# A new hand-written order for an attention and mixture-of-experts kernel on one core

## The chip, the core and the metric

One core of one Trainium2 chip runs the whole program in one launch. The metric is device microseconds of that launch, as the median of several runs. Engines are named as the profile names them: PE is TensorE's matmuls, PEld its weight loads, DVE is VectorE, ACT is ScalarE, POOL is GpSimd, SP is the engine that starts most of the DMA transfers.

## The reference

Three layers follow one another. All arrays are float32.

```python
# 1. attention: batch 4, 8 heads, 576 positions, head width 64, each query sees 64 keys
scores = (q @ k.T) / 8, masked to 0 <= i - j < 64, minus the row's maximum
attn   = exp(scores) / (sum + 1e-9)
x      = (attn @ v), heads side by side          # 2304 tokens x 512
# 2. a dense layer of width 2048
h = x @ w_in
x = (max(h, 0) + alpha * min(h, 0)) @ w_out      # 2304 x 512
# 3. eight experts of width 1024, the best one for each token
e   = argmax(x @ w_gate), gate = softmax(x @ w_gate)[e]
out = gate * (max(x @ w1[e], 0) @ w2[e])
```

## The kernel before, in words

Float32 products are made of three matmuls on a pair of a rounded operand ("hi") and the rest ("lo"): hi by hi, hi by lo and lo by hi. So each operand is first split by two instructions, a rounding copy and a subtraction.

The tokens are 18 tiles of 128, in five blocks of 4, 4, 4, 3 and 3 tiles. One attention *group* is half of the heads of one tile, so a block of 4 tiles needs groups 0 to 7, the next one groups 8 to 15, and so on up to 35. The dense layer runs block by block, over 16 slices f of 128 of its width. Its 16 weight tiles (`wcat`, 1 MB each, both weight matrices of a slice) are loaded once, and each is prepared once by six instructions before block 0 can use it. The experts' part follows after the last block.

**The order is written out by hand.** `PLAN` (line 29) is a list of tokens, a letter and a number, and `play` (line 834) issues one step for each. Every engine executes its own instructions in the order in which they stand there, and waits at the first one whose operands are not ready. The plan covers blocks 0 to 3; the last block and the experts have loops of their own. The tokens:

- `X`g loads group g's queries, keys and values (SP, line 248); `W`f loads weight tile f (SP, line 179); `c` loads constants.
- `S`g scores (PE, line 279, with two mask matmuls before it, line 273); `x`g row maxima (DVE, 290); `y`g scales them by 1/8 (294); `e`g four exponentials (ACT, 301); `q`g adds epsilon to the sums (309); `r`g reciprocal (DVE, 313); `n`g normalises the probabilities (DVE, 321, or four instructions on ACT, 319); `T`g transposes them (PE, 327); `P`g copies them out of PSUM (337); `O`g multiplies them with the values (PE, 351); `H`g and `L`g split the result into hi (ACT, 337) and lo (DVE, 364).
- `0`f to `5`f prepare weight tile f: `0` scales its exponent words (ACT, 191), `1`, `2`, `3` put the bits together (DVE, 195, 199, 203), `4` rounds to hi (ACT, 337), `5` subtracts for lo (DVE, 211). So `13` is step 1 of tile 3 and `110` step 1 of tile 10.
- In block j, with i = 16 j + f: `s`i is the first product of slice f (PE, 376 to 378, 12 matmuls), `R`, `t` its activation (ACT 391, DVE 395), `h`, `l` the split of that (ACT 337, DVE 401), `u`i the second product (PE, 418 to 420).
- `B`n is n matmuls whose result nobody reads (PE, line 261), `b8` the eight at the very start.
- `Z`, `N`, `D`, `G`, `J`, `j`, `M`, `I`, `i` belong to the routing of finished blocks; `N` loads a row of the gate's weights (`wge`, SP, line 465), `D` is a product with it (DVE, 474).

A suffix names the engine where it is not the usual one: `d` DVE, `p` POOL, `a` ACT. The usual engine of `y`, `q` and `n` is DVE, that of `P` is ACT.

What ties the steps together beyond their data: from group 8 on, `S`, `T` and `O` share two PSUM banks (`aslot`, `give`): `S` takes both and `e` gives them back, `T` takes one until `P`, `O` takes one until `L`. `s` has two banks (`h`), so s2 waits for t0. `raw` has two buffers, so X7 waits for O0 and X9 for O7. Weight tile 8 is loaded over the raw words of tile 0, so W8 waits for `50`.

```python
    def w_low(f):
        lo, hi = wpart(f)
        DVE.tensor_scalar(out=lo, in0=lo, scalar1=29, scalar2=None, op0=ALU.logical_shift_right)
    def out_lo(g):
        xh, xl = xt_part(g)
        DVE.tensor_tensor(out=xl, in0=ob.pop(g).rearrange(...), in1=f32(xh), op=ALU.subtract)
        give(("O", g))
```

Of the kernel before, what the change touches and what calls it, by code (L numbers as in the profile page):

```python
# [28 lines left out]
PLAN = """
c0 X0 b8 X1 c1 S0 X2 B2 x0 S1 y0 C0 e0 W0 B7 x1 y1 e1 S2 q0 r0 X3 n0 x2 T0 B2 P0d y2p X4 00 q1 O0 r1 n1 e2 10 T1 X5 S3  # L30
20 B2 P1d W1 H0 S4 q2p x3 O1 L0 y3p r2 e3 B2 n2 X6 x4 T2 B2 P2d y4p 30 O2 H1 q3p X7 e4 S5 L1 r3 B3 n3 W2 x5 T3 H2 q4p
S6 40 P3d y5p L2 O3 r4 e5 n4 B1 W3 x6 T4 B2 P4d y6p 50 O4 H3 q5p e6 X8 S7 L3 B3 r5 n5 W4 x7 T5 H4 q6p B4 01 L4 y7p P5d
r6 e7 O5 n6 W5 11 T6 B7 21 H5 q7p P6 31 W6 02 O6 L5 B4 r7 H6 n7 41 L6 T7 12 W7 B7 03 51 P7 22 04 O7 W8 B7 32 H7 05 L7
42 13 s0 X9 23 06 52 07 W9 S8 33 R0 s1 08 t0 W10 x8 h0 43 14 y8p s2 l0 e8 53 24 W11 u0 R1 q8p 34 09 r8 t1 44 W12 15 S9
n8a 54 s3 h1 x9 010 l1 y9p 25 R2 u1 e9 t2 35 s4 16 h2 q9p 45 r9 l2 26 n9a T8 55 u2 P8 R3 36 011 t3 46 O8 17 T9 27 X10
H8 s5 h3 P9 L8 l3 012 56 R4 O9 37 u3 H9 X11 L9 47 t4 18 h4 S10 57 s6 l4 x10 R5 t5 y10p e10 u4 28 38 h5 q10p 19 S11 48
r10 l5 s7 n10a 58 x11 W13 R6 29 y11p u5 e11 t6 39 h6 q11p T10 110 49 s8 l6 r11 P10 n11 R7 59 013 O10 t7 W14 u6 H10 210
h7 L10 310 X12 T11 s9 l7 410 111 P11 510 R8 014 t8 O11 211 u7 H11 X13 h8 L11 311 S12 112 411 l8 s10 x12 R9 511 y12p
e12 t9 u8 212 h9 q12p 312 S13 r12 412 n12 s11 l9 512 R10 t10 W15 u9 x13 h10 113 y13p e13 213 s12 l10 313 R11 q13p 015
r13 n13 T12 413 t11 u10 114 P12 513 h11 214 O12 T13 H12 X14 l11 s13 P13 L12 R12 314 t12 414 O13 115 h12 u11 514 X15  # L40
H13 L13 215 S14 l12 s14 315 R13 x14 415 t13 y14p e14 u12 515 h13 q14p r14 S15 n14 l13 s15 x15 R14 t14 y15p e15 u13 h14
q15p r15 n15 T14 l14 T15 P14 u14 P15 R15 t15 h15 O14 l15 O15 H14 X16 u15 L14 H15 L15 X17 s16 Z0 Z1 N0 Z2 N1 Z3 S16 R16
s17 D0 t16 x16 h16 s18 l16 y16 R17 D1 e16 t17 u16 D2 D3 h17 q16 N2 r16 n16 S17 D4 s19 l17 x17 R18 y17 t18 e17 u17 D5
D6 D7 h18 T16 q17 N3 r17 l18 s20 P16 n17 R19 D8 D9 O16 D10 u18 H16 X18 D11 L16 t19 N4 D12 h19 T17 D13 s21 P17 l19 D14
R20 D15 t20 O17 N5 u19 D16 h20 X19 H17 D17 L17 D18 D19 S18 s22 l20 N6 x18 R21 y18 t21 e18 u20 D20 D21 D22 h21 S19 q18
r18 n18 s23 l21 x19 R22 u21 y19 D23 e19 t22 N7 D24 D25 s24 h22 q19 r19 n19 l22 D26 R23 T18 D27 T19 P18 u22 t23 P19 D28
h23 D29 D30 O18 l23 O19 H18 X20 D31 R24 u23 L18 H19 t24 X21 L19 h24 G0 s25 S20 l24 s26 x20 R25 y20 t25 e20 u24 h25 q20
r20 n20 S21 l25 s27 x21 R26 y21 t26 e21 u25 h26 q21 r21 n21 T20 J0 l26 P20 s28 j0 R27 O20 u26 H20 X22 L20 M0 t27 T21
I0 P21 s29 i0 h27 M1 l27 R28 O21 t28 I1 H21 X23 u27 L21 h28 i1 S22 l28 s30 x22 R29 y22 t29 e22 u28 h29 q22 r22 n22 S23
l29 s31 x23 R30 y23 t30 e23 u29 h30 q23 r23 n23 T22 l30 T23 P22 u30 P23 R31 t31 h31 O22 l31 O23 H22 X24 u31 L22 H23  # L50
L23 X25 s32 Z4 Z5 N8 Z6 N9 Z7 S24 R32 s33 D32 t32 x24 h32 s34 l32 y24 R33 D33 e24 t33 u32 D34 D35 h33 q24 N10 r24 n24
S25 D36 s35 l33 D37 R34 D38 t34 u33 D39 h34 x25 N11 y25 s36 D40 e25 l34 D41 D42 R35 T24 q25 u34 r25 P24 n25 t35 D43
h35 D44 N12 O24 l35 T25 H24 X26 D45 s37 R36 P25 L24 D46 D47 t36 O25 N13 u35 D48 h36 X27 H25 D49 L25 D50 D51 S26 s38
l36 N14 x26 R37 y26 t37 e26 u36 D52 D53 D54 h37 S27 q26 r26 l37 s39 n26 R38 D55 t38 N15 D56 u37 h38 D57 D58 D59 s40
l38 x27 R39 t39 u38 y27 h39 D60 e27 D61 D62 s41 l39 D63 R40 q27 r27 n27 T26 t40 u39 P26 G1 h40 O26 T27 H26 X28 s42 P27
L26 l40 R41 t41 O27 h41 u40 X29 H27 L27 S28 l41 s43 x28 R42 y28 t42 e28 u41 h42 q28 r28 n28 J1 l42 T28 j1 s44 R43 P28
O28 u42 H28 X30 M2 L28 t43 I2 s45 h43 i2 M3 l43 R44 I3 u43 t44 i3 h44 S29 l44 s46 x29 R45 y29 t45 e29 u44 h45 q29 r29
n29 s47 l45 R46 t46 h46 T29 u45 P29 O29 l46 H29 X31 u46 R47 L29 t47 h47 s48 l47 u47 R48 t48 h48 S30 Z8 l48 s49 Z9 x30
N16 Z10 N17 Z11 y30 u48 e30 D64 D65 s50 D66 R49 q30 r30 n30 S31 t49 D67 s51 h49 l49 N18 x31 R50 u49 t50 y31 h50 D68
e31 s52 l50 D69 D70 u50 D71 R51 q31 N19 r31 n31 T30 t51 T31 D72 P30 s53 P31 D73 h51 D74 l51 O30 D75 R52 O31 X32 H30  # L60
t52 u51 H31 L30 h52 L31 X33 D76 s54 D77 l52 N20 D78 R53 u52 D79 t53 N21 h53 D80 S32 l53 s55 x32 R54 y32 D81 u53 e32
D82 D83 t54 N22 S33 q32 h54 r32 s56 n32 l54 x33 R55 u54 y33 D84 e33 D85 D86 D87 T32 q33 N23 r33 P32 n33 O32 t55 T33
D88 h55 X34 s57 H32 l55 P33 L32 R56 D89 t56 O33 D90 u55 h56 X35 H33 D91 L33 D92 S34 l56 s58 x34 R57 u56 y34 t57 e34
D93 D94 s59 D95 h57 q34 r34 l57 n34 S35 R58 t58 u57 x35 h58 s60 y35 l58 e35 G2 u58 R59 T34 P34 t59 J2 q35 O34 h59 r35
n35 s61 H34 l59 L34 R60 j2 u59 T35 P35 t60 O35 M4 h60 s62 H35 L35 l60 I4 R61 u60 i4 t61 M5 h61 s63 l61 R62 t62 u61 h62
I5 l62 i5 u62 R63 t63 h63 l63
"""
# [977 lines left out]
```

## Time and profile before

| | |
|---|---|
| median of 3 runs (lowest, highest) | 781.07 us (781.02, 781.63) |
| the profiled execution's own time | 780.53 us |
| its span, first to last instruction | 778.7 us |
| PE busy | 759.4 us (98%) |
| PEld, DVE, ACT, POOL busy | 611.9, 622.6, 461.3, 76.6 us |
| granted TensorE clock, mean | 0.997 of full speed |
| matmuls and their records | 4590 |

The program runs attention for block 0 first (to about 38 us), then the dense layer of blocks 0 to 3 with the attention of the next block in between, then the last block (to about 478 us) and the experts. A PE that is shown busy is not always at its peak, since a matmul's pipeline is counted in; how far apart matmuls start says more. Times in timelines are the start from the span's begin and the length of one group of instructions; in square brackets stands the idle time before it and who ended it.

### The profile page before, as it was taken

What the parts mean: (1) busy time and instruction counts of PE and PEld (TensorE: products, weight loads), DVE (VectorE), ACT (ScalarE), POOL (GpSimd) and SP (SyncE); (2) the same over time, 40 slices, a digit from 0 to 9 for tenths busy, and PEclk for the clock granted to TensorE, in tenths of its full rate; (3) what the DMA queues carried; (4) which work ended last, traced back from release to release, by engine and by line L of the source; (5) the groups of instructions that cost most, each with busy time, mean ns of one, the idle gap of its engine ahead of it and who ended that gap; (6) DMA issues with size and microseconds to landing.
All of it is one profiled execution on the core that took longest, in us unless ns stands there. A gap on an engine that the chain in (4) does not pass through costs nothing.

```text
span 778.7 us, 12731 instructions
## 1 busy us (share of the span) xinstructions
PE 759.4 (98%) x4590; PEld 611.9 (79%) x4595; DVE 622.6 (80%) x1267; ACT 461.3 (59%) x892; POOL 76.6 (10%) x80
## 2 busy tenths in 40 slices
...
GB/s 362 406 355 75 156 82 75 76 92 65 130 75 101 29 129 103 65 65 27 117 89 109 48 48 136 216 178 27 41 281 247 28 218 293 264 257 248 194 88 51
DMA packets 24259, 109.91 MB, mean 141 GB/s; under 512 B 3006, under 2 KB 3390, under 8 KB 17024
## 3 DMA queue, kind: packets, MB, share of 16 engines
...
HBM read 154.09 MB, written 10.26 MB: 211 GB/s over the span
## 4 chain that ended last, share of the span: by engine, by line
PE 81%; DVE 9%; DMA 6%; issue 2%; ACT 1%; SPq 0%; DVEq 0%
PE acc L737 12%; PE h L376 8%; PE acc L418 8%; PE acc L419 8%; PE acc L420 8%; PE h L377 8%; PE h L378 8%; DVE hl L819 4%; PE h L709 4%; PE h L711 4%; PE h L710 4%; DMA hl<-in_wcat_dram 2%; PE att L351 2%; DMA hl<-in_qkv_dram 2%; PE att L279 2%
## 5 line engine op out<-in xcount | busy, mean ns | idle before, releaser
L819 DVE TENSOR_TENSOR hl<-hl,hl 128x1024 fp32r<-128x1024 f32 x176 | 211.2, 1222 | 16.7 <-ACT hl L813 16.0
L813 ACT CAST hl<-hl 128x1024 fp32r<-128x1024 f32 x176 | 180.2, 1049 | 3.6 <-DMA hl<-in_wx_dram 2.6
L737 PE MATMUL acc<-hl,xl 128*128 128x512 f32 x504 | 130.7, 400 | 2.5 <-DVE xl L724 2.5
L376 PE MATMUL h<-xh,hl 128*128 128x512 f32 (+1 forms) x320 | 122.9, 384 | 0.8 <-DVE g L395 0.8
L378 PE MATMUL h<-xh,hl 128*128 128x512 f32 (+1 forms) x320 | 118.0, 369 | 0.0
L377 PE MATMUL h<-xl,hl 128*128 128x512 f32 (+1 forms) x320 | 118.0, 369 | 0.0
L419 PE MATMUL acc<-hl,gl 128*128 128x512 f32 x288 | 112.9, 392 | 0.4 <-DVE gl L401 0.4
L420 PE MATMUL acc<-hl,gh 128*128 128x512 f32 x288 | 112.8, 392 | 0.0
L391 ACT ACTIVATE g<-h 128x512 f32<-128x512 f32 (+1 forms) x80 | 44.6, 558 | 112.7 <-DVE gl L401 99.2
L418 PE MATMUL acc<-hl,gh 128*128 128x512 f32 x288 | 109.8, 401 | 0.0
L737 PEld LDWEIGHTS acc<-hl,xl 128*128 128x128 f32 x504 | 91.2, 188 | 21.4 <-DVE xl L724 3.8
L401 DVE TENSOR_TENSOR gl<-g,gh 128x512 fp32r<-128x512 f32 (+1 forms) x80 | 50.8, 636 | 58.9 <-PE acc L419 54.1
...
L474 DVE SCALAR_TENSOR_TENSOR dot<-stage,wge 128x512 bf16<-128x512 f32 x96 | 66.0, 688 | 10.0 <-DMA wge<-in_wgt_dram 7.6
L337 ACT CAST gh<-g 128x512 fp32r<-128x512 f32 (+1 forms) x80 | 46.5, 581 | 45.9 <-DVE g L395 42.8
L376 PEld LDWEIGHTS h<-xh,hl 128*128 128x128 f32 x320 | 60.1, 188 | 14.0 <-issue 4.0
L395 DVE SCALAR_TENSOR_TENSOR g<-g,beta,h 128x512 f32<-128x512 f32 (+1 forms) x80 | 55.0, 688 | 16.3 <-ACT g L391 16.1
L709 PE MATMUL h<-hl,xh 128*128 128x512 f32 x168 | 67.6, 403 | 0.0
L378 PEld LDWEIGHTS h<-xh,hl 128*128 128x128 f32 x320 | 60.1, 188 | 8.1
L711 PE MATMUL h<-hl,xh 128*128 128x512 f32 x168 | 66.1, 393 | 0.4 <-DVE xh L697 0.2
L377 PEld LDWEIGHTS h<-xl,hl 128*128 128x128 f32 x320 | 60.2, 188 | 7.4
L710 PE MATMUL h<-hl,xh 128*128 128x512 f32 x168 | 65.5, 390 | 0.0
...
## 6 DMA issues: line engine op xcount, KB each, us to landing
...
```

What stands on the lines that cost most here:

```text
L376: PE.matmul(out=h[:, 0:n], lhsT=w_in_op(f, k, 0), rhs=xh[:, k, :], start=(k == 0), stop=False)
L377: PE.matmul(out=h[:, 0:n], lhsT=w_in_op(f, k, 0), rhs=xl[:, k, :], start=False, stop=False)
L378: PE.matmul(out=h[:, 0:n], lhsT=w_in_op(f, k, 1), rhs=xh[:, k, :], start=False, stop=(k == 3))
L418: PE.matmul(out=a, lhsT=gh[:, c0:c0 + 128], rhs=w_out_op(f, 0), start=(f == 0), stop=False)
L419: PE.matmul(out=a, lhsT=gl[:, c0:c0 + 128], rhs=w_out_op(f, 0), start=False, stop=False)
L420: PE.matmul(out=a, lhsT=gh[:, c0:c0 + 128], rhs=w_out_op(f, 1), start=False, stop=(f == 15))
L709: PE.matmul(out=o, lhsT=th[:, k, :], rhs=wh, start=(k == 0), stop=False)
L710: PE.matmul(out=o, lhsT=th[:, k, :], rhs=wl, start=False, stop=False)
L711: PE.matmul(out=o, lhsT=tl[:, k, :], rhs=wh, start=False, stop=(k == 3))
L737: PE.matmul(out=o, lhsT=x[:, f % 4, :], rhs=w[:, lo, (f % 2) * 512:(f % 2) * 512 + 512], start=(x is th and f == 0 and lo == 0), stop=(x i ...
L813: ACT.copy(out=t[:, 0, :], in_=r)
L819: eng.tensor_tensor(out=t[:, 1, :], in0=r, in1=f32(t[:, 0, :]), op=ALU.subtract)
```

## The change

Nothing but the text of `PLAN` changes: 1141 tokens become 1137, and nearly all of them up to the end of block 3 stand in a new order (the five last alone keep their place). By kinds:

- `y`2 to `y`15 and `q`2 to `q`15 (14 and 14 instructions of 128x4) go from POOL to DVE.
- `P`1 to `P`5, copies of 128x512, go from DVE to ACT (`P`0 stays on DVE).
- `n`11 to `n`14 go from DVE to ACT. With `n`8, `n`9 and `n`10, which were there, seven normalisations are on ACT.
- Of the `B` matmuls, 55 in 15 tokens become 51 in 11 (`b8` stays).
- All else is order. The diff, cut to its first lines and to those that the text speaks of:

```diff
-c0 X0 b8 X1 c1 S0 X2 B2 x0 S1 y0 C0 e0 W0 B7 x1 y1 e1 S2 q0 r0 X3 n0 x2 T0 B2 P0d y2p X4 00 q1 O0 r1 n1 e2 10 T1 X5 S3
-20 B2 P1d W1 H0 S4 q2p x3 O1 L0 y3p r2 e3 B2 n2 X6 x4 T2 B2 P2d y4p 30 O2 H1 q3p X7 e4 S5 L1 r3 B3 n3 W2 x5 T3 H2 q4p
-S6 40 P3d y5p L2 O3 r4 e5 n4 B1 W3 x6 T4 B2 P4d y6p 50 O4 H3 q5p e6 X8 S7 L3 B3 r5 n5 W4 x7 T5 H4 q6p B4 01 L4 y7p P5d
-r6 e7 O5 n6 W5 11 T6 B7 21 H5 q7p P6 31 W6 02 O6 L5 B4 r7 H6 n7 41 L6 T7 12 W7 B7 03 51 P7 22 04 O7 W8 B7 32 H7 05 L7
-42 13 s0 X9 23 06 52 07 W9 S8 33 R0 s1 08 t0 W10 x8 h0 43 14 y8p s2 l0 e8 53 24 W11 u0 R1 q8p 34 09 r8 t1 44 W12 15 S9
-n8a 54 s3 h1 x9 010 l1 y9p 25 R2 u1 e9 t2 35 s4 16 h2 q9p 45 r9 l2 26 n9a T8 55 u2 P8 R3 36 011 t3 46 O8 17 T9 27 X10
...
-h7 L10 310 X12 T11 s9 l7 410 111 P11 510 R8 014 t8 O11 211 u7 H11 X13 h8 L11 311 S12 112 411 l8 s10 x12 R9 511 y12p
...
-D82 D83 t54 N22 S33 q32 h54 r32 s56 n32 l54 x33 R55 u54 y33 D84 e33 D85 D86 D87 T32 q33 N23 r33 P32 n33 O32 t55 T33
...
-D93 D94 s59 D95 h57 q34 r34 l57 n34 S35 R58 t58 u57 x35 h58 s60 y35 l58 e35 G2 u58 R59 T34 P34 t59 J2 q35 O34 h59 r35
-n35 s61 H34 l59 L34 R60 j2 u59 T35 P35 t60 O35 M4 h60 s62 H35 L35 l60 I4 R61 u60 i4 t61 M5 h61 s63 l61 R62 t62 u61 h62
...
+c0 X0 b8 X1 c1 S0 X2 B2 x0 S1 y0 C0 e0 W0 B7 x1 y1 e1 S2 q0 r0 n0 X3 x2 T0 B3 P0d X4 00 q1 O0 r1 n1 H0 y2 T1 10 e2 X5
+S3 L0 20 B4 W1 x3 P1 S4 q2 r2 O1 n2 y3 H1 T2 x4 X6 e3 B8 L1 y4 30 X7 P2 S5 q3 r3 n3 e4 O2 11 W2 T3 x5 B2 y5 H2 S6 q4
+r4 P3 n4 e5 W3 O3 L2 x6 T4 B3 y6 12 H3 S7 X8 P4 q5 L3 e6 r5 O4 n5 x7 T5 W4 B6 y7 13 H4 q6 P5 L4 r6 e7 O5 n6 W5 T6 B7
+H5 q7 r7 P6 n7 W6 01 O6 L5 14 T7 H6 B3 21 P7 40 O7 L6 W7 B6 31 H7 02 L7 50 S8 41 X9 22 s0 03 W8 51 04 x8 05 s1 y8 32
+R0 W9 e8 t0 23 33 h0 S9 42 l0 43 q8 u0 r8 52 R1 x9 n8a W10 t1 s2 y9 h1 53 e9 l1 W11 24 u1 R2 q9 r9 34 06 W12 n9a t2 T8
+15 s3 25 P8 h2 35 44 O8 l2 45 T9 X10 54 u2 H8 R3 L8 P9 t3 07 55 O9 h3 s4 16 X11 H9 l3 08 L9 26 09 u3 36 R4 010 t4 46
...
+e11 t6 W13 19 h6 q11 T10 r11 29 n11a s8 l6 P10 39 R7 013 O10 t7 u6 110 X12 H10 h7 210 49 L10 310 T11 P11 l7 410 O11 59
...
+l54 T32 D84 R55 u54 P32 t55 D85 h55 D86 O32 s57 l55 H32 X34 D87 R56 L32 t56 N23 S33 D88 h56 u55 x33 s58 y33 l56 e33
+D89 D90 u56 D91 R57 q33 r33 n33 S34 t57 D92 s59 h57 l57 x34 R58 u57 y34 t58 e34 D93 s60 D94 D95 h58 q34 r34 T33 n34
+P33 l58 T34 G2 O33 R59 P34 u58 X35 H33 O34 H34 L33 L34 J2 t59 j2 s61 h59 l59 S35 M4 R60 u59 x35 y35 t60 e35 s62 h60
+q35 r35 I4 n35 l60 T35 i4 u60 R61 M5 P35 t61 O35 h61 I5 l61 H35 s63 L35 R62 i5 t62 h62 u61 l62 u62 R63 t63 h63 l63
```

## Rows read from the trace of the kernel before

**Rows 1.** Busy time by stretch: PE, PEld, DVE, ACT, POOL, then PE clock, DMA share, GB/s.

```profile
10.00:45.00 35.00, 31.73 (x352) 19.85 (x355) 32.52 (x60) 26.53 (x78) 2.90 (x12) 1.00 1.01 411
...
60.00:120.00 60.00, 60.00 (x394) 47.05 (x393) 55.08 (x74) 37.90 (x83) 5.85 (x8) 1.00 0.31 104
120.00:380.00 260.00, 260.00 (x1709) 208.84 (x1708) 175.88 (x472) 98.94 (x280) 0.91 (x4) 1.00 0.25 84
```

**Rows 2.** Timeline of PE: first and third matmul of s0, S8, then the first of s1 and s3.

```profile
38.65 0.58 PE L376 MATMUL h<-xh,hl 128*128 128x512 f32 x1
...
39.30 0.39 PE L378 MATMUL h<-xh,hl 128*128 128x512 f32 x1
...
41.59 0.39 PE L273 MATMUL att<-c 128*128 128x256 bf16 x2
...
42.51 0.50 PE L376 MATMUL h<-xh,hl 128*128 128x512 f32 x1
...
52.89 0.50 PE L376 MATMUL h<-xh,hl 128*128 128x512 f32 x1 [0.55 <-DVE g L395]
```

**Rows 3.** Timeline of SP: transfers issued: two rows of the gate, then X7.

```profile
8.67 1.85 SPq L465 DMA_DIRECT2D wge<-in_wgt_dram  x2
13.16 0.33 SPq L248 DMA_DIRECT2D raw<-in_qkv_dram  x1
```

**Rows 4.** Timeline of ACT: steps 05 and 06, and the normalisation n8a.

```profile
38.30 1.19 ACT L191 ACTIVATE hl<-hl 128x1024 f32<-128x1024 f32 x1 [0.50 <-DMA hl<-in_wcat_dram]
...
40.80 1.19 ACT L191 ACTIVATE hl<-hl 128x1024 f32<-128x1024 f32 x1 [0.28 <-DMA hl<-in_wcat_dram]
...
53.19 1.28 ACT L319 ACTIVATE sm<-sm,rs 128x128 f32<-128x128 f32 x4
```

**Rows 5.** Timeline of DVE: r0; x6; then n7, L6, 12, 51, 22, 32.

```profile
10.04 0.18 DVE L313 RECIPROCAL rs<-rs 128x4 f32<-128x4 f32 x1
...
23.95 0.75 DVE L290 TENSOR_REDUCE nm<-acc 128x2 f32<-128x256 f32 x2
...
33.85 0.69 DVE L321 TENSOR_TENSOR sm<-sm,rs 128x512 f32<-128x512 f32 x1
34.46 0.42 DVE L364 TENSOR_TENSOR xl<-att,xh 128x256 fp32r<-128x256 f32 x1
34.80 0.68 DVE L195 TENSOR_SCALAR hl<-hl 128x1024 int32<-128x1024 int32 x1
35.40 1.22 DVE L211 TENSOR_TENSOR hl<-hl,hl 128x1024 fp32r<-128x1024 f32 x1
36.53 1.22 DVE L199 SCALAR_TENSOR_TENSOR hl<-hl 128x1024 int32<-128x1024 int32 x1
37.78 1.23 DVE L203 SCALAR_TENSOR_TENSOR hl<-hl 128x1024 int32<-128x1024 int32 x1
```

**Rows 6.** Timeline of PE: T8 with u2 behind it; T32 with O32; O34 behind T34.

```profile
61.23 0.60 PE L327 MATMUL att<-c,sm 128*128 128x128 f32 x4
61.59 0.47 PE L418 MATMUL acc<-hl,gh 128*128 128x512 f32 x1
...
389.04 0.60 PE L327 MATMUL att<-c,sm 128*128 128x128 f32 x4
390.31 0.69 PE L351 MATMUL att<-pt,raw 128*64 128x64 f32 x16 [0.68 <-ACT pt L337]
...
412.13 0.69 PE L351 MATMUL att<-pt,raw 128*64 128x64 f32 x16 [0.34 <-ACT pt L337]
```

**Rows 7.** Timeline of PE: fillers at the start, and two more a little later.

```profile
1.32 3.60 PE L261 MATMUL h<-zero 128*128 128x512 bf16 x8 [1.32 <-POOL one L853]
...
6.42 0.61 PE L261 MATMUL h<-c 128*128 128x512 bf16 x2
```

**Rows 8.** Busy time by stretch at the end, columns as in Rows 1.

```profile
770.00:772.00 2.00, 1.22 (x6) 0.66 (x4) 2.00 (x4) 1.72 (x4) 1.27 (x1) 1.00 0.00 0
...
774.00:776.00 2.00, 0.00 (x0) 0.00 (x0) 0.18 (x1) 0.00 (x0) 0.00 (x0) 0.57 0.47 137
```

More of the change, by code (lines that the diff above doesn't have):

```diff
@@ L35 @@
-n8a 54 s3 h1 x9 010 l1 y9p 25 R2 u1 e9 t2 35 s4 16 h2 q9p 45 r9 l2 26 n9a T8 55 u2 P8 R3 36 011 t3 46 O8 17 T9 27 X10
-H8 s5 h3 P9 L8 l3 012 56 R4 O9 37 u3 H9 X11 L9 47 t4 18 h4 S10 57 s6 l4 x10 R5 t5 y10p e10 u4 28 38 h5 q10p 19 S11 48
-r10 l5 s7 n10a 58 x11 W13 R6 29 y11p u5 e11 t6 39 h6 q11p T10 110 49 s8 l6 r11 P10 n11 R7 59 013 O10 t7 W14 u6 H10 210
-h7 L10 310 X12 T11 s9 l7 410 111 P11 510 R8 014 t8 O11 211 u7 H11 X13 h8 L11 311 S12 112 411 l8 s10 x12 R9 511 y12p
-e12 t9 u8 212 h9 q12p 312 S13 r12 412 n12 s11 l9 512 R10 t10 W15 u9 x13 h10 113 y13p e13 213 s12 l10 313 R11 q13p 015
@@ L40 @@
[L40 to L59, printed above, removed]
@@ L60 @@
-e31 s52 l50 D69 D70 u50 D71 R51 q31 N19 r31 n31 T30 t51 T31 D72 P30 s53 P31 D73 h51 D74 l51 O30 D75 R52 O31 X32 H30
-t52 u51 H31 L30 h52 L31 X33 D76 s54 D77 l52 N20 D78 R53 u52 D79 t53 N21 h53 D80 S32 l53 s55 x32 R54 y32 D81 u53 e32
-D82 D83 t54 N22 S33 q32 h54 r32 s56 n32 l54 x33 R55 u54 y33 D84 e33 D85 D86 D87 T32 q33 N23 r33 P32 n33 O32 t55 T33
-D88 h55 X34 s57 H32 l55 P33 L32 R56 D89 t56 O33 D90 u55 h56 X35 H33 D91 L33 D92 S34 l56 s58 x34 R57 u56 y34 t57 e34
-D93 D94 s59 D95 h57 q34 r34 l57 n34 S35 R58 t58 u57 x35 h58 s60 y35 l58 e35 G2 u58 R59 T34 P34 t59 J2 q35 O34 h59 r35
@@ L65 @@
-n35 s61 H34 l59 L34 R60 j2 u59 T35 P35 t60 O35 M4 h60 s62 H35 L35 l60 I4 R61 u60 i4 t61 M5 h61 s63 l61 R62 t62 u61 h62
-I5 l62 i5 u62 R63 t63 h63 l63
+c0 X0 b8 X1 c1 S0 X2 B2 x0 S1 y0 C0 e0 W0 B7 x1 y1 e1 S2 q0 r0 n0 X3 x2 T0 B3 P0d X4 00 q1 O0 r1 n1 H0 y2 T1 10 e2 X5
+S3 L0 20 B4 W1 x3 P1 S4 q2 r2 O1 n2 y3 H1 T2 x4 X6 e3 B8 L1 y4 30 X7 P2 S5 q3 r3 n3 e4 O2 11 W2 T3 x5 B2 y5 H2 S6 q4
+r4 P3 n4 e5 W3 O3 L2 x6 T4 B3 y6 12 H3 S7 X8 P4 q5 L3 e6 r5 O4 n5 x7 T5 W4 B6 y7 13 H4 q6 P5 L4 r6 e7 O5 n6 W5 T6 B7
@@ new lines @@
+H5 q7 r7 P6 n7 W6 01 O6 L5 14 T7 H6 B3 21 P7 40 O7 L6 W7 B6 31 H7 02 L7 50 S8 41 X9 22 s0 03 W8 51 04 x8 05 s1 y8 32
+R0 W9 e8 t0 23 33 h0 S9 42 l0 43 q8 u0 r8 52 R1 x9 n8a W10 t1 s2 y9 h1 53 e9 l1 W11 24 u1 R2 q9 r9 34 06 W12 n9a t2 T8
+15 s3 25 P8 h2 35 44 O8 l2 45 T9 X10 54 u2 H8 R3 L8 P9 t3 07 55 O9 h3 s4 16 X11 H9 l3 08 L9 26 09 u3 36 R4 010 t4 46
+17 S10 27 h4 s5 011 l4 x10 012 y10 56 e10 u4 37 18 R5 q10 s6 r10 47 t5 28 n10a 57 S11 h5 38 s7 l5 48 x11 R6 y11 58 u5
+e11 t6 W13 19 h6 q11 T10 r11 29 n11a s8 l6 P10 39 R7 013 O10 t7 u6 110 X12 H10 h7 210 49 L10 310 T11 P11 l7 410 O11 59
@@ new lines @@
+u7 X13 H11 R8 510 W14 L11 t8 S12 111 h8 s9 x12 y12 l8 e12 211 u8 311 R9 014 q12 r12 t9 S13 n12a 112 212 s10 h9 x13 411
+l9 y13 u9 511 e13 312 R10 113 T12 412 q13 s11 r13 t10 P12 213 n13a 512 O12 h10 T13 313 W15 H12 s12 P13 L12 413 l10 114
+R11 X14 513 O13 u10 H13 t11 X15 015 L13 214 h11 S14 314 s13 x14 414 y14 l11 e14 514 u11 115 R12 215 q14 r14 S15 t12
+n14a 315 s14 h12 x15 415 l12 y15 u12 R13 515 e15 t13 s15 h13 q15 r15 n15 l13 R14 T14 t14 T15 P14 u13 P15 h14 O14 l14
+O15 H14 X16 R15 u14 L14 H15 t15 X17 L15 h15 s16 l15 u15 R16 t16 h16 S16 Z0 l16 s17 Z1 x16 N0 Z2 N1 Z3 y16 e16 u16 D0
@@ new lines @@
+D1 D2 R17 q16 r16 s18 n16 t17 D3 h17 D4 N2 T16 l17 s19 P16 D5 R18 D6 t18 O16 D7 h18 u17 D8 H16 X18 L16 D9 N3 D10 S17
+D11 s20 l18 N4 x17 R19 y17 u18 t19 e17 D12 D13 D14 h19 S18 q17 r17 s21 n17 l19 x18 R20 u19 y18 t20 e18 D15 D16 N5 s22
+D17 h20 q18 l20 r18 R21 n18 t21 T17 T18 D18 h21 u20 P17 D19 P18 D20 N6 D21 D22 O17 l21 O18 H17 X19 s23 D23 R22 H18 L17
+L18 X20 t22 D24 h22 u21 N7 D25 D26 D27 S19 l22 s24 x19 R23 y19 t23 e19 u22 D28 D29 D30 h23 q19 r19 n19 S20 s25 l23 x20
+R24 y20 t24 e20 u23 D31 G0 h24 T19 s26 P19 q20 r20 n20 O19 l24 T20 H19 X21 u24 R25 L19 P20 t25 h25 O20 l25 J0 H20 X22
@@ new lines @@
+u25 R26 j0 s27 L20 t26 M0 h26 S21 s28 x21 y21 l26 e21 u26 R27 q21 r21 n21 t27 I0 T21 i0 s29 h27 M1 P21 l27 R28 O21 t28
+I1 H21 X23 u27 i1 h28 L21 S22 l28 s30 x22 R29 y22 t29 e22 u28 h29 q22 r22 n22 S23 l29 s31 x23 R30 y23 t30 e23 u29 h30
+q23 r23 n23 T22 l30 T23 P22 u30 P23 R31 t31 h31 O22 l31 O23 H22 X24 u31 L22 H23 L23 X25 s32 Z4 Z5 N8 Z6 N9 Z7 S24 R32
+s33 D32 t32 x24 h32 s34 l32 y24 R33 D33 e24 t33 u32 D34 D35 h33 q24 N10 r24 n24 S25 D36 s35 l33 D37 R34 D38 t34 u33
+D39 h34 x25 N11 s36 y25 l34 e25 D40 D41 D42 R35 u34 q25 t35 r25 h35 n25 D43 T24 l35 N12 T25 P24 D44 s37 P25 D45 R36
@@ new lines @@
+D46 t36 O24 D47 h36 u35 X26 H24 D48 L24 D49 N13 D50 O25 l36 s38 H25 X27 D51 R37 L25 t37 N14 D52 h37 u36 D53 D54 D55
+S26 D56 N15 s39 l37 x26 R38 y26 t38 u37 e26 D57 D58 D59 h38 S27 q26 r26 n26 s40 l38 x27 R39 u38 t39 y27 h39 D60 e27
+D61 D62 s41 l39 q27 R40 r27 n27 t40 T26 D63 h40 u39 P26 G1 O26 T27 H26 X28 s42 P27 L26 l40 R41 t41 O27 u40 h41 X29 H27
+L27 J1 l41 s43 j1 R42 u41 t42 M2 h42 S28 s44 x28 y28 l42 e28 u42 R43 q28 r28 n28 t43 I2 T28 i2 s45 h43 M3 P28 l43 R44
+O28 t44 I3 H28 X30 u43 i3 h44 L28 S29 l44 s46 x29 R45 y29 t45 e29 u44 h45 q29 r29 n29 s47 l45 R46 t46 h46 T29 u45 P29
```

4 lines of the change are left out of this document (added).

## The prediction

> **What bounds the kernel now.** I read the busy times by stretch first, then the timeline of each engine up to 60 us, then PE's timeline for every place where two matmuls start further apart than their work. From 60 to 380 us PE is busy in all of it, at full clock [rows 1]. Its matmuls of 512 columns start 0.229 us apart (from 39.30 to 41.59 are ten of them) [rows 2], so one `s` or `u` of block 0 takes 12 x 0.229 = 2.74 us. The plan can therefore move the end in two ways alone: when the dense layer gets going, and the few holes that PE has later. I found three of the second kind: O32, O34 and O35, each waiting for the copy of the transpose just before it (two rows stand for them; O35 shows the 0.68 us idle of O32 again) [rows 6].
>
> Before 45 us no engine is free. The DMA share is 1.01 and DVE works 32.52 of 35 us [rows 1]: the transfers are one full queue, and DVE has the attention of block 0 and the first weight tiles to do. s0 starts at 38.65, and s3 at 52.89, when PE has done s0, s1, s2, u0, S8 and S9 [rows 2]. I measure the new order against that set.
>
> **The change, part by part.** *Moved work.* 28 small steps (`y`, `q`) come to DVE. Each is like the reciprocal, 0.18 us [rows 5]: 28 x 0.18 = 5.0 us. Five copies of 128x512 leave; I take n7's 0.61 us from start to start [rows 5] for each, 3.1 us. Four normalisations leave too, 4 x 0.61 = 2.4 us, and cost ACT 4 x 1.28 us [rows 4], where 22 of 60 us are idle from 60 on [rows 1]. DVE's sum hardly changes (-0.5 us). The four missing `B` matmuls stand where PE waits anyway: nothing. POOL loses its 28 steps and nothing there waits for them. On SP, X9 now goes ahead of W8, and W8 waits for `50` at 40.7; the queue before them is full to 43.3 (W7, one tile after W6's 40.8), so X9 lands at 45.0 and W8 at 47.5, where S9 and `08` come later: nothing, or 1 us at most should `09` and `010` press. What remains is order.
>
> *Weights against the order.* SP's order of transfers is the same in both plans through W7. A weight tile takes 40.80 - 38.30 = 2.50 us, W5 landing at 38.30 [rows 4]; a group's tile is 704 KB against 1024, so 1.72 us. Back from W5, in the order X7 W2 W3 X8 W4 W5: W4 lands at 35.8, W3 at 31.6, W2 at 29.1, X7 at 26.6. Before, step `12` (the first on tile 2) starts at 34.80 [rows 5], long after. In the new order it stands right behind x6 and y6. x6 started at 23.95 [rows 5], released by X6's landing, which does not move; with 0.75 us for it and 0.2 for y6, DVE stands at `12` at 24.8 and waits to 29.1, 4.3 us. Queued behind: q5 r5 n5, x7, `13`, and so T5, S8 and all later groups. This wait swallows whatever the moved copies gained ahead of it, so I count from 29.1 with starts from row to row (`12` 0.60, W steps 1.13 to 1.25, `L` 0.34, `n` 0.61) [rows 5]: q5 29.7, n5 30.3, x7 30.9, y7 31.7, `13` 31.8, n6 33.0, q7 33.8 (after e7), n7 34.2, L5 34.9; then `14` waits for W4, 35.8; `21` 36.5, L6 37.6, `31` 38.0, L7 39.15, `50` 39.5 to 40.7.
>
> *Start of the dense layer.* S8 now stands ahead of s0 and needs the bank that L7 gives back: 39.6, and takes 42.51 - 41.59 = 0.92 [rows 2], so s0 starts at 40.5. s0 and s1 end at 46.0. On ACT five steps on weight tiles stand between H7 and R0, of 1.19 us each with a tenth of overlap [rows 4]; H7 is done at 38.8, so R0 ends at 44.8. e8 follows with its four parts, so S9 gets its banks at 46.3. On DVE t0, `23` and `33` stand before l0, done at 48.8; u0's second matmul waits for it, so u0 ends at 51.3 and s2 at 54.05. Against 52.89: **1.2 us later**. Each of some six hand-offs may be 0.2 off, and PE's wait at l0 may be smaller by 1.4: -0.2 to +2.4.
>
> *Later holes.* T32 and T35 now have a `u` between them and their products. From T to O it takes 390.31 - 389.04 = 1.27 us, of which the transposes need 61.59 - 61.23 = 0.36: 0.91 saved twice. O34 gets a `u` as well, where 0.34 idle and a tail of 0.17 are shown: 0.5 [rows 6]. T33, T34 and O33 now follow one another: 1.27 - 2 x 0.36 = 0.55 lost. Together **-1.8** (bounds -2.3 and -0.9, if n34 is late for T34). One new hole: T11 and O11 stand side by side, where s9 stood between them: **+0.9**.
>
> *Sum.* 1.2 + 0.9 - 1.8 = +0.3 us against 780.53 of the profiled execution (span 778.7), which lies 0.54 under the median of 781.07. So 781.4 as a median. Bounds -0.2 + 0.9 - 2.3 = -1.6 and 2.4 + 0.9 - 0.9 = +2.4: this case's own range is 779.5 to 783.5.
>
> **The rivals.** *PE falls to half clock (slower).* O4 ends at 27.4 (X7's landing, S7, O4), and T5 needs n5, done at 31.0: PE stands still 3.6 us, right before the dense layer. Before, fillers and groups left no such hole. At the end of the trace PE's work stops at 771.2 (1.22 us of that stretch), and the granted clock, 1.00 to 774, is 0.57 on average from 774 to 776 [rows 8], so it fell about 3.1 us after the last matmul. The first fillers started 3.60/8 = 0.45 us apart, twice as far as those from 6.42 on [rows 7]: 1.2 GHz, and some 5 us of work until 2.4. If it falls in the new hole, 5 us from T5 on run at half, 2.5 us of work lost, of which 0.9 falls into waits for P5 and n6: +1.6, so 783.0, and up to 784.2 if none does. It decides if the clock falls before 31.0. The Trainium skill ("TensorE: Matmul & The Clock Gate", "Why this matters for your kernels") says the same of any kernel: no idle stretches between bursts of matmuls, or the array is back at half rate. By that rule the sum would be +1.9 rather than +0.3. I keep full clock as the likelier, since the groups on both sides of the hole are activity and the row shows one fall only.
>
> *The gate's rows no longer travel ahead of X7.* Two transfers of 256 KB that belong behind Z0 were issued between X6 and X7 [rows 3]. If the new order leaves them where they belong, everything above comes 2 x 256/1024 x 2.50 = 1.25 us sooner: 780.1. For it: their place is not in the plan. Against it: X7 still waits for O0, which is where they slipped in.
>
> *DVE stays behind.* At the reference set DVE has `24`, `34` and `15` still to do (2.9 us) but l1 and x9 done (1.3): 1.6 us more debt, less 0.2 of moved steps. Idle in 60 to 120 us are 60 - 55.08 = 4.9 us [rows 1], which should take it up. The first test is u2: l2 is done at 60.7, PE is there at 61.1. If DVE can't use its idle time, the debt of 1.4 shows: 782.8.
>
> **How the numbers follow.** About 0.2% (1.56 us) is what a measurement of this kernel tells from no change: faster is under 779.5, slower over 782.6. Forecast 0.43 (faster 0.04, same 0.34, slower 0.05); half clock 0.33 (0, 0.04, 0.29); gate's rows 0.16 (0.08, 0.08, 0); DVE's debt 0.08 (0, 0.02, 0.06). Sums: 0.12, 0.48, 0.40. The range 778.8 to 784.2 runs from the gate's case less its hand-offs to the clock's upper end.
>
> **What would show it.** On DVE a `12` with some 4 us idle before it, ended by a weight tile's transfer, and a smaller one at `14`. PE idle ahead of T5; the granted clock between 25 and 45 us says which case it is. s0 at 40.5, u0 with a wait for l0, u1 at 54.0. T11 to O11 1.27 us apart, no hole at O32 and O35. I am wrong if W2 is there before DVE wants it: then s0 comes at about 36, and the kernel gains some 4 us.

## The result, and the profile after

| | before | after |
|---|---|---|
| median, beside each other on one chip | 781.17 us (5 runs) | 785.29 us (784.31 to 786.09, 5 runs) |
| ratio, 95% interval | | 1.0054 (1.0043 to 1.0064) |
| profiled execution, span | 780.53 us, 778.7 us | 784.31 us, 782.5 us |
| granted TensorE clock, mean | 0.997 | 0.995 |

The kernel became 4.1 us slower; the forecast was 781.4 and its range ended at 784.2. Lines of the kernel after have numbers lower by one. From here on a *hole* is the time by which two matmuls start further apart than the work of the first one.

First the busy times by stretch of the kernel after, columns as in [rows 1], with three short stretches of the start below:

```profile
10.00:45.00 35.00, 29.35 (x340) 18.66 (x340) 27.43 (x63) 24.09 (x79) 0.00 (x0) 0.95 0.99 396
60.00:120.00 60.00, 59.33 (x400) 46.35 (x399) 54.79 (x79) 43.64 (x94) 0.00 (x0) 1.00 0.32 113
...
25.00:30.00 5.00, 1.76 (x36) 1.07 (x33) 0.74 (x3) 2.01 (x10) 0.00 (x0) 1.00 1.00 404
30.00:35.00 5.00, 3.78 (x24) 2.05 (x26) 4.20 (x15) 1.99 (x9) 0.00 (x0) 0.66 1.02 429
35.00:40.00 5.00, 4.97 (x61) 3.08 (x56) 4.07 (x6) 3.79 (x6) 0.00 (x0) 1.00 1.01 421
```

From 10 to 45 us DVE worked 27.4 us instead of 32.5, with the transfers as full as before. In five of these microseconds it worked 0.74. And from 30 to 35 us the clock stood at 0.66 on average, which is 2.4 GHz for a part of it and 1.2 GHz for the rest. What DVE waited for stands in its timeline, where the rows are `y6` and `12`:

```profile
24.60 0.17 DVE L293 TENSOR_SCALAR nm<-nm 128x4 f32<-128x4 f32 x1
29.26 0.70 DVE L194 TENSOR_SCALAR hl<-hl 128x1024 int32<-128x1024 int32 x1 [4.49 <-DMA hl<-in_wcat_dram]
```

PE's timeline after, in this order: O4, T5, fillers; s0; the first two matmuls of u0; u1; T11 and O11; then in block 3 T33 with T34, O33, s61 and S35:

```profile
27.41 0.69 PE L350 MATMUL att<-pt,hl 128*64 128x64 f32 x16
31.22 1.12 PE L326 MATMUL att<-c,sm 128*128 128x128 f32 x4 [3.13 <-DVE sm L320]
32.13 2.51 PE L260 MATMUL h<-c 128*128 128x512 bf16 x6
...
42.06 0.50 PE L375 MATMUL h<-xh,hl 128*128 128x512 f32 x1
...
48.56 0.51 PE L417 MATMUL acc<-hl,gh 128*128 128x512 f32 x1
50.11 0.50 PE L418 MATMUL acc<-hl,gl 128*128 128x512 f32 x1 [1.05 <-DVE gl L400]
...
55.46 0.39 PE L417 MATMUL acc<-hl,gh 128*128 128x512 f32 x1
...
94.07 0.60 PE L326 MATMUL att<-c,sm 128*128 128x128 f32 x4
95.34 0.69 PE L350 MATMUL att<-pt,raw 128*64 128x64 f32 x16 [0.67 <-ACT pt L336]
...
408.63 1.04 PE L326 MATMUL att<-c,sm 128*128 128x128 f32 x8
409.91 0.69 PE L350 MATMUL att<-pt,raw 128*64 128x64 f32 x16 [0.24 <-ACT pt L336]
...
414.93 0.45 PE L375 MATMUL h<-xh,hl 128*128 128x384 f32 x1 [1.01 <-DVE g L394]
...
418.24 0.67 PE L278 MATMUL att<-raw 64*64 64x128 f32 x16 [0.93 <-DMA raw<-in_qkv_dram]
```

PE stands still for 3.13 us ahead of T5, and the six fillers behind it take 2.51 us: the half clock. u1 starts at 55.46, where the kernel before had done the same set at 52.89 [rows 2]: 2.6 us late. T11 and O11 are 1.27 us apart. The holes of before at O32, O34 and O35 [rows 6] are gone, but block 3 has three others: 0.6 us at O33 (1.28 us from T33, of which the eight transposes need 2 x 0.36), 1.2 at s61, 1.1 at S35. The first is in the forecast; the other two come from orders of other engines. DVE after, L34 and t59:

```profile
413.93 0.42 DVE L363 TENSOR_TENSOR xl<-att,xh 128x256 fp32r<-128x256 f32 x1 [2.36 <-ACT xh L336]
414.27 0.60 DVE L394 SCALAR_TENSOR_TENSOR g<-g,beta,h 128x384 f32<-128x384 f32 x1
```

t59 frees the bank that s61 needs. It now stands behind L34, for which DVE waited 2.36 us. And SP after, where the 1 MB store of a finished block leaves just ahead of X35:

```profile
410.77 0.38 SPq L501 DMA_DIRECT2D x1d<-stage  x1
411.24 2.31 SPq L247 DMA_DIRECT2D raw<-in_qkv_dram  x1
```

The row of the kernel before that answers to it is this one, two loads in one group, X34 and X35:

```profile
391.04 3.93 SPq L248 DMA_DIRECT2D raw<-in_qkv_dram  x2
```

X35 waits for O33, since `raw` has two buffers. O33 moved back in the plan, so X35 went out some 16 us later, behind the store. Its issue takes 2.31 us there, where a load in [rows 3] shows 0.33; no run tells apart what the late O33 and the store each add to the hole at S35.

### The profile page after: what moved, and what is told of

The parts are those of the page before. It is cut to its first block, busy times and chain, and to the rows that moved or that the text cites. A ratio compares the mean times of both kernels' runs of the same rounds, so it can differ in the third digit from the quotient of the medians.

```text
span 782.5 us, 12742 instructions
## 1 busy us (share of the span) xinstructions
PE 760.0 (97%) x4591; PEld 612.8 (78%) x4591; DVE 621.7 (79%) x1286; ACT 467.2 (60%) x913; POOL 63.8 (8%) x52
## 4 chain that ended last, share of the span: by engine, by line
PE 84%; DVE 8%; DMA 5%; issue 2%; ACT 1%; SPq 0%
PE acc L736 12%; PE h L375 9%; PE acc L417 8%; PE acc L418 8%; PE acc L419 8%; PE h L377 8%; PE h L376 8%; DVE hl L818 4%; PE h L708 4%; PE h L710 4%; PE h L709 4%; PE att L350 2%; PE att L278 2%; DMA hl<-in_wcat_dram 2%; PE att L326 2%
```

## The experiments

Each was timed in turns with the kernel before on the same chip; ratios are to that one, with 95% intervals. Diffs show the tokens of the plan that moved.

**1. The weight steps late.** The kernel after, with `12`, `13` and `14` taken out of the start:

```diff
-x6 T4 B3 y6 12 H3 S7 ... B6 y7 13 H4 ... O6 L5 14 T7 ... X9 22 s0 ... t0 23 33 ... W11 24 u1
+x6 T4 B3 y6 H3 S7 ... B6 y7 H4 ... O6 L5 T7 ... X9 12 22 s0 ... t0 13 23 33 ... W11 14 24 u1
```

> The new order with one thing taken back: steps 12, 13 and 14 stand directly ahead of 22, 23 and 24 instead of among the groups' steps. Theory (VectorE stands at a weight tile that has not landed): the idle time of 4.5 us ahead of 12 and the hole of PE ahead of T5 are gone, the clock stays at 1.00, s0 starts at 36 to 38 us instead of 42.1, and u1, which waits on ScalarE's step 05 (W5 lands at 38.4) and on VectorE, at 50 to 52 instead of 55.5. The time is 779.5 to 782.0 us against 785.3 of the new order. Rival (the moved steps cost it, two engines now carry more): nothing of the moved work is undone, so the time stays at 784 or more.

Measured: 781.96 us (12 runs), 1.0017 (1.0007 to 1.0027), 3.3 us less than the change. The hole ahead of T5 is gone and s0 comes at 36.91. But PE then stops at S9. PE's timeline of this kernel: s0, then S9 and matmuls of u0 behind it:

```profile
36.91 0.50 PE L375 MATMUL h<-xh,hl 128*128 128x512 f32 x1
...
45.37 0.67 PE L278 MATMUL att<-raw 64*64 64x128 f32 x16 [2.46 <-DMA raw<-in_qkv_dram]
45.97 0.50 PE L417 MATMUL acc<-hl,gh 128*128 128x512 f32 x1
46.47 0.50 PE L418 MATMUL acc<-hl,gl 128*128 128x512 f32 x1
...
47.06 0.63 PE L417 MATMUL acc<-hl,gh 128*128 128x512 f32 x1
```

X9 landed only now; its place in the queue of transfers is the same as in the change, where the forecast had it land at 45.0. So a dense layer that starts 5 us sooner waits there, and the clock falls again: from 47.06 on the matmuls are 0.63 us long instead of 0.39. The step `12` was the cause of the first stop, and most of what its removal won was given back at the next load.

**2. Fillers in the hole.** The kernel after, with fifteen unread matmuls for PE to run while DVE waits:

```diff
-r5 O4 n5 x7 T5
+r5 O4 B15 n5 x7 T5
```

> The new order with 15 more unread matmuls between O4 and T5, 15 x 0.215 = 3.2 us of PE work in the hole of 3.1 us idle. VectorE's wait at 12 stays as it is. Theory: the granted clock stays at 1.00 from 25 to 45 us and s0 starts 1.3 to 1.9 us sooner, at 40.2 to 40.8; the time falls by as much, to 783.4 to 784.0, and no further. Rival (the clock costs nothing, since VectorE sets the pace up to s0 anyway): s0 stays at 42.0 and the time at 785.3.

Measured: 783.43 us (782.83 to 783.55, 7 runs), 1.0028 (1.0017 to 1.0039), 1.9 us less than the change. Busy time by stretch (columns as in [rows 1]):

```profile
30.00:35.00 5.00, 4.89 (x41) 2.73 (x39) 4.66 (x15) 2.78 (x12) 0.00 (x0) 1.00 1.02 426
```

PE's timeline of this kernel, s0 and u1:

```profile
40.69 0.50 PE L375 MATMUL h<-xh,hl 128*128 128x512 f32 x1
...
54.10 0.39 PE L417 MATMUL acc<-hl,gh 128*128 128x512 f32 x1
```

At full clock s0 and u1 stand where the forecast's sum had put them, at 40.5 and 54.05. So the half clock costs 1.9 us by the medians; at u1 the two traces are 1.4 us apart (55.46 against 54.10).

**3. One token alone.** The kernel before, with only `12` moved up:

```diff
-W3 x6 T4 B2 ... L6 T7 12 W7 B7
+W3 x6 12 T4 B2 ... L6 T7 W7 B7
```

> The kernel before with one token moved: 12 stands directly behind x6, as in the new order. No step changes its engine. Theory: VectorE waits there from about 24.7 to 29.2 us, 4 us of its work before s0 are lost, PE gets a hole ahead of T5, s0 comes at 41 to 43 instead of 38.65, and the time is 783.5 to 786.5. Rival (order of one step is nothing, the moved work is what counts): 781.2.

Measured: 786.66 us (5 runs), 1.0069 (1.0056 to 1.0082). Its timeline of PE, O4 and s0, and the busy time by stretch:

```profile
30.74 1.12 PE L350 MATMUL att<-pt,hl 128*64 128x64 f32 x16 [5.06 <-DVE pt L336]
...
45.70 0.58 PE L375 MATMUL h<-xh,hl 128*128 128x512 f32 x1
```

```profile
30.00:35.00 5.00, 4.04 (x38) 2.65 (x40) 4.02 (x9) 1.41 (x2) 0.23 (x1) 0.50 1.01 426
```

This one token costs 5.5 us, more than the whole change. In the order of before the copy P4 is on DVE and so is caught behind the wait as well; PE stops for 5.06 us, and the clock stands at 1.2 GHz for all of 30 to 35 us. That the change, with these copies on ACT, loses less with the same token does not show that the copies soften the wait: experiment 4 has them on DVE again, in the new order.

**4. The engines as before.** The order after, but every moved step on its old engine:

```diff
-y2 ... q2 ... P1 ... n11a
+y2p ... q2p ... P1d ... n11
```

> The new order with every step back on the engine it had before: y and q 2 to 15 on GpSimd, P1 to P5 and n11 to n14 on VectorE. Theory: the wait for W2 at 12 hides whatever that costs or gains ahead of it, so the time stays within 1 us of the new order's 785.3, and VectorE's idle time ahead of 12 shrinks by 1 to 2 us without s0 coming sooner. Rival (the moved steps cost it): most of the loss goes, 781 to 782.5.

Measured: 785.68 us (5 runs), 1.0058 (1.0045 to 1.0071), the same as the change. In the new order, with its wait at `12`, it does not matter which engine does the 28 small steps, five copies and four normalisations. Whether it would without that wait was not tried.

**5. S9 late too.** From experiment 1, so that no step on PE stands ahead of data that come later; on DVE and ACT some weight steps move back behind the dense layer's as well:

```diff
-R0 W9 e8 t0 13 23 33 h0 S9 42 l0 43 q8 u0 r8 52 R1 x9 n8a W10 t1 s2 y9 h1 53 e9 l1
+R0 W9 e8 t0 h0 l0 42 q8 u0 r8 52 R1 W10 t1 13 s2 23 n8a h1 S9 l1 33 43 x9 y9 53 e9
```

> The kernel after with 12, 13, 14 late (as in the first experiment), and S9 moved from ahead of u0 to behind s2; on DVE l0 and t1 go ahead of 13, 23, 33, and on ACT 43 goes behind h1. My theory (every early loss is PE standing at the first step of its queue whose data come late: before it was 12, now S9 waiting for X9 and u0 waiting for l0): u0 starts at about 43.3 instead of 45.97, no hole over 1 us and full clock from 33 us on, s2 at about 46.6, u1 at 50.2 to 51.5, s3 at about 53, where the first experiment had u1's end at about 56; so some 3 us less than its 781.96: 778.8 (778 to 780.2). Rival, the early part is bound by the transfers or by the sum of DVE's work, and the wait turns up elsewhere (s3 waiting for 33, 43, 53, or s2 for 52): 781.5 to 782.5, with PE idle ahead of s2 or s3.

Measured: 783.42 us (7 runs), 1.0032 (1.0021 to 1.0044), 1.5 us more than experiment 1. u0 came at 43.67 as expected, and then u2 stopped. DVE's timeline, three weight steps and l2; then PE's row of u2 and the busy time by stretch:

```profile
56.73 0.69 DVE L194 TENSOR_SCALAR hl<-hl 128x1024 int32<-128x1024 int32 x1
57.45 1.23 DVE L198 SCALAR_TENSOR_TENSOR hl<-hl 128x1024 int32<-128x1024 int32 x1
58.71 1.23 DVE L202 SCALAR_TENSOR_TENSOR hl<-hl 128x1024 int32<-128x1024 int32 x1
59.86 0.68 DVE L400 TENSOR_TENSOR gl<-g,gh 128x512 fp32r<-128x512 f32 x1
```

```profile
60.60 0.50 PE L418 MATMUL acc<-hl,gl 128*128 128x512 f32 x1 [2.15 <-DVE gl L400]
```

```profile
60.00:65.00 5.00, 4.40 (x21) 3.15 (x23) 5.00 (x7) 3.93 (x6) 0.00 (x0) 0.69 0.29 112
```

l2 waits for nothing but its turn: `15`, `25` and `35` of a slice that PE wants much later stand ahead of it. My theory for this run missed that queue. Whether it is the order, or DVE's whole work that is too much, experiment 11 tells apart.

**6. T11 and O11 apart.** From experiment 2:

```diff
-T11 P11 l7 410 O11 59 u7 X13
+T11 P11 l7 410 59 u7 O11 X13
```

> The kernel after with the filler of the second experiment (B15 between O4 and T5, full clock throughout), and O11 moved from right behind T11 to behind u7. My theory: the 1.27 us from T11 to O11 become 0.36, and the hole is 0.9 us of pure loss: 0.9 us less than the second experiment's 783.43, so 782.5. Rival (such a hole is taken up later, since PE then waits for DVE or for transfers anyway): 783.4, with the 0.9 us turning up as idle time before a later matmul.

Measured: 782.92 us (9 runs), 1.0026 (1.0016 to 1.0036), where experiment 2 has 1.0028: no gain that can be told. The hole at O11 is gone, and PE's timeline has another one, in the masks of S12:

```profile
97.84 0.27 PE L272 MATMUL att<-c 128*128 128x256 bf16 x1 [0.71 <-DVE xl L363]
```

S12 needs both banks, and O11 gives its own back only with L11, which is now later too. The rival was right: the hole moved to the next user of what O11 holds.

**7. The old block 3 in the new kernel.** From experiment 2, with the order of before from u50 on.

> The second experiment's kernel up to u50, then the order of before for the rest of block 3. My prediction as put on record: the old order costs 1.8 us more there (holes at O32, O34, O35), so 785.2. My theory now, from the two traces: the new order removed those three holes and made three others (O33 behind T33 and T34; s61 behind an L34 that waits in DVE's queue; S35 behind an X35 issued late), about 0.8 us more in sum; so 782.6. The holes of the other plan should show at O32, O34 and O35 and nowhere else in block 3.

Measured: 783.13 us (10 runs), 1.0030 (1.0020 to 1.0039), the same as experiment 2. PE's timeline shows the old holes back, at O32, O34 and O35, and one at T33 that was not expected and that the timeline of before does not have:

```profile
392.86 0.69 PE L350 MATMUL att<-pt,raw 128*64 128x64 f32 x16 [0.68 <-ACT pt L336]
394.13 0.65 PE L326 MATMUL att<-c,sm 128*128 128x128 f32 x4 [0.59 <-DVE sm L320]
...
415.18 0.69 PE L350 MATMUL att<-pt,raw 128*64 128x64 f32 x16 [0.34 <-ACT pt L336]
...
421.33 0.69 PE L350 MATMUL att<-pt,raw 128*64 128x64 f32 x16 [0.68 <-ACT pt L336]
```

The gain of 1.8 us that the prediction gave to the new block 3 is not there.

**8. Only the three holes.** The kernel before, with a `u` put into each hole of [rows 6] and nothing else moved:

```diff
-R55 u54 y33 ... T32 q33 N23 r33 P32 n33 O32 ... G2 u58 R59 T34 P34 t59 J2 q35 O34 ... u59 T35 P35 t60 O35
+R55 y33 ... T32 q33 N23 r33 P32 u54 n33 O32 ... G2 R59 T34 P34 t59 J2 u58 q35 O34 ... T35 P35 u59 t60 O35
```

> The kernel before with only three tokens moved: u54 to behind P32, u58 to behind J2, u59 to behind P35, so that a u stands between each transpose and its product, and O33, X35 and L34 keep their places. My theory (the idea of the new block 3 is right, its loss comes from what else was moved with it): the three holes of 0.91, 0.5 and 0.9 us go and none comes: 2.3 us less than before, about 778.8 (ratio 0.997). Rival (O32, O34, O35 wait for n or for P whatever stands between, or the time comes back at the next hand-off): 781.1, ratio 1.000, with holes of the same sum in block 3.

Measured: 780.57 us (11 runs), 0.9993 (0.9984 to 1.0002): half a microsecond, hardly to be told from nothing. The holes at O34 and O35 are gone. The one at O32 went to T32, which without u54 ahead of it waits for the bank that the exponentials e33 give back:

```profile
388.14 0.66 PE L326 MATMUL att<-c,sm 128*128 128x128 f32 x4 [1.05 <-ACT sm L300]
```

**9. Another filling for O32.** From experiment 8, with u54 back in its place and s57 in the hole:

```diff
-y33 D84 e33 D85 D86 D87 T32 q33 N23 r33 P32 n33 O32 t55 T33 D88 h55 X34 s57 H32 l55 P33 L32
+y33 t55 D84 e33 h55 T32 P32 q33 r33 n33 D85 D86 D87 N23 s57 O32 l55 T33 X34 H32 P33 D88 L32
```

> The kernel before with u58 and u59 moved as in the experiment before this, u54 back in its old place, and the hole between T32 and O32 filled with s57 instead; for that the activation t55 (whose bank s57 takes) and n33 go ahead of three gate products D85, D86, D87 on DVE. My theory (in the last experiment T32 only waited for the bank that e33 gives back, and t55 still came at 390.9 us because DVE, which works 9.7 of 10 us there, had four gate products ahead of it): all three holes go, none comes, 2.3 us less than before: 778.7 (778.2 to 779.2). Rival (DVE is the bound from 380 to 396 us, so what is put behind t55 comes late instead): only the holes at O34 and O35 count, 1.4 us less than before, 779.6, with PE waiting for an l, an L or an n between 390 and 400 us.

Measured: 782.18 us (11 runs), 1.0019 (1.0010 to 1.0028), slower than before. Both theories missed: the hole at O32 is filled, but one of its size stands at O33, from ahead of which s57 was taken; and X34, which waits for O32, left at 393.01 instead of 391.04. PE waits for it at S34. PE's timeline, O33 and S34, then SP's, X34 and X35:

```profile
394.09 0.69 PE L350 MATMUL att<-pt,raw 128*64 128x64 f32 x16 [0.68 <-ACT pt L336]
...
399.12 0.67 PE L278 MATMUL att<-raw 64*64 64x128 f32 x16 [2.06 <-DMA raw<-in_qkv_dram]
```

```profile
393.01 2.13 SPq L247 DMA_DIRECT2D raw<-in_qkv_dram  x2
```

It is the mechanism of X35 and S35 in the kernel after, in another place: the product O releases a load.

**10. The new block 3 alone.** The order of before up to u50, that of after from there on.

> The order of before up to u50 and the order of after from there on: the new block 3 by itself, without the new start. My prediction on record (the new order of block 3 is worth 1.8 us): 779.2. My theory now (it takes three holes of 2.3 us in sum out and puts 2.4 to 3.1 us of others in: O33 0.8, s61 1.2, S35 0.4 to 1.1): 781.0 to 781.9, with these three holes in the trace and none at O32, O34, O35.

Measured: 781.76 us (11 runs), 1.0006 (0.9997 to 1.0015), 0.7 us above before. PE's timeline has the holes of the kernel after at O33 (0.6 us as there, not the 0.8 of the text), s61 and S35:

```profile
407.70 0.69 PE L350 MATMUL att<-pt,raw 128*64 128x64 f32 x16 [0.24 <-ACT pt L336]
...
412.71 0.44 PE L375 MATMUL h<-xh,hl 128*128 128x384 f32 x1 [1.01 <-DVE g L394]
...
416.01 0.67 PE L278 MATMUL att<-raw 64*64 64x128 f32 x16 [0.94 <-DMA raw<-in_qkv_dram]
```

**11. l2 first.** From experiment 5 (the text below speaks of it as three experiments back):

```diff
-t2 T8 15 s3 25 P8 h2 35 44 O8 l2 45 T9 X10 54 u2 H8 R3 L8 P9 t3 07 55 O9 h3 s4 16 X11 H9 l3 08
+t2 T8 15 s3 P8 h2 l2 44 O8 25 T9 X10 H8 P9 54 u2 L8 35 R3 45 t3 O9 h3 55 s4 07 l3 16 X11 H9 08
```

> The kernel with late weights and late S9 (three experiments back, 783.42 us), in which u2 waited 2.15 us for l2 and the clock fell behind that wait. Here l2 goes ahead of 25 and 35 on DVE, 54 directly behind 25, and H8, P9 ahead of 45 on ACT. My theory (order alone: DVE reached l2 late because weight steps stood ahead of it that PE wants later): no hole at u2, full clock from 33 us on, u3 about 3.8 us sooner: 779.6 (779 to 780.5), below before. Rival (block 0 is bound by the sum of DVE's work, which every weight tile needs before its slice): the 2.4 us turn up ahead of s4, s5 or u4 instead, and the time stays at 782.5 to 783.5.

Measured: 780.58 us (779.29 to 781.88, 11 runs), 0.9993 (0.9984 to 1.0002), 2.8 us less than experiment 5. The stop at u2 is gone, none of its size comes after it, and the clock stays up in the stretch where it fell:

```profile
60.00:65.00 5.00, 4.84 (x34) 3.48 (x33) 4.47 (x7) 3.47 (x5) 0.00 (x0) 1.00 0.65 229
```

So it was the order of DVE's queue, not the sum of its work. The gain over the kernel before could not be shown: the interval holds 1.

**12. Together.** Experiment 11, T11 moved to behind O10 (O11 stays where it is), and the order of before from u50 on with u58 and u59 moved as in experiment 8:

```diff
-O10 t7 u6 110 X12 H10 h7 210 49 L10 310 T11 P11 l7 410 O11
+O10 T11 t7 u6 110 X12 H10 P11 h7 210 49 L10 310 l7 410 O11
```

> The early part of the experiment before this (late weights, late S9, l2 first; 780.58 us), with T11 moved from ahead of O11 to behind O10 so that u6 stands between T11 and O11, and from u50 on the order of before with u58 and u59 moved behind J2 and P35. My theory (each hole left there is plain loss as long as the product O itself stays in its place, since the transfers X wait for it): 1.0 us for T11, 0.7 us for the new block 3 against the old one, 1.4 us for O34 and O35: 777.5 (777 to 778.5), faster than before. Rival (what is won early is given back where DVE or a transfer sets the pace, as at S12, S34 and S35 in the other runs): 779.5 to 780.5, with PE waiting for a transfer or for DVE somewhere between 90 and 420 us.

Measured: 778.73 us (778.12 to 779.29, 9 runs), 0.9971 (0.9961 to 0.9981): faster than before by 2.3 us and than the change by 6.5 (the ratio of the two ratios is 0.9917). There is no hole at O11, S12, O34, O35, s61 or S35. Of the expected gain 1.2 us are missing. PE's timeline has the hole of the old block 3 at O32, which no move was to fill, and one more at T33, which waits 0.58 us for n33 as in experiment 7; what the rest is stays open:

```profile
389.08 0.69 PE L350 MATMUL att<-pt,raw 128*64 128x64 f32 x16 [0.68 <-ACT pt L336]
390.34 0.66 PE L326 MATMUL att<-c,sm 128*128 128x128 f32 x4 [0.58 <-DVE sm L320]
```

## Why the prediction was wrong, step by step

**The early wait was right.** DVE was to stand at `12` from 24.8 to 29.1, 4.3 us; it waited 4.49 us, to 29.26. With the clock up (experiment 2) s0 and u1 came at 40.69 and 54.10, forecast 40.5 and 54.05. Experiment 3 shows that the token by itself is enough for it. The start's **+1.2** stands.

**Moved work at nothing was right** for this order: experiment 4. **T11 beside O11, +0.9, was right in the trace** (1.27 us apart). That it is worth 0.9 us of the end, no run shows by itself: in experiment 6 the time moved on to S12.

**First step that failed: later holes, -1.8.** The prediction counted which tokens stand next to each T and O, and found the three old holes filled, which they are, and 0.55 us lost at O33, where 0.56 were. It did not follow what the moved steps release or hold up: X35 waits for O33, t59 stands behind L34. These two holes, S35 and s61, are 2.3 us in the profiled run of after, as much as the three old ones together; the new block 3 costs 0.7 us (experiment 10, interval -0.2 to 1.2), and experiments 8 and 9 show that the old holes can't be had for the asking either. The term was off by 2.5 us. Its bounds, -2.3 and -0.9, did not reach to a loss at all, because nothing was counted that might come beside O33.

**Second step that failed: the clock.** The half-clock rival, with 0.33, is what happened. "I keep full clock as the likelier, since the groups on both sides of the hole are activity and the row shows one fall only" was the wrong choice: the row [rows 8] spoke for a fall after a stop of this size, and nothing measured spoke against it. (The stop itself was forecast at 3.6 us and is 3.13, since O4 ends at 28.1 and not at 27.4.) The rule of the Trainium skill that the prediction cited ("TensorE: Matmul & The Clock Gate", "Why this matters for your kernels"), that idle stretches between bursts bring the half rate back, agrees with the trace here: granted clock 0.66 from 30 to 35 us. The price was nearly right, +1.6 forecast, 1.9 measured as the difference of experiment 2's median from the change's. In part that is luck: the prediction put 5 us from T5 on at half clock, but T5 starts at 31.22 and the row of 35 to 40 us shows full clock again, so that 3.8 us are the most there can be.

**The sum.** 1.2 for the start, 0.9 for T11, 1.9 for the clock and 0.7 for block 3 make 4.7 us, where 4.1 were measured; the 0.6 between lies within the intervals of the parts. The range failed because the two errors were treated as cases of their own: its upper end, 784.2, was the clock's worst case with the full -1.8 still in it. (The working gives 781.4 + 2.5 = 783.9 for that case; for the other 0.3 it names no term.)

**The other rivals.** The gate's rows still travel ahead of X7, as SP's timeline of the kernel after shows:

```profile
8.40 1.89 SPq L464 DMA_DIRECT2D wge<-in_wgt_dram  x2
12.91 0.33 SPq L247 DMA_DIRECT2D raw<-in_qkv_dram  x1
```

DVE's debt does not show: from 60 to 120 us PE is busy 59.33 of 60 us, and the 0.67 us missing is the idle time at O11. The sentence on being wrong, that with W2 there in time s0 comes at about 36, is what experiment 1 built: 36.91. But the 4 us of gain that it promised were not there, since S9 had a wait of its own behind, and with S9 moved back, in experiment 5, u2 had one.
